# Twenty-six weight units of a dense expert layer: five closing additions and splits issued between second-layer tiles, with pinned queue order

## The chip, the cores and the metric

The kernel runs on one core of a Trainium2 chip. The metric is the device time of one execution in microseconds. The core has a TensorE (PE; its weight loads are shown apart as PEld), a VectorE (DVE), a ScalarE (ACT), a GpSimd (POOL) and a SyncE (SP), which here issues the loads from DRAM. Each engine works through a queue of its own in order.

## What is computed

The reference, cut to what matters:

```python
x = attention(q, k, v)                  # block-causal, 4 x 8 heads, 576 x 64 -> x: 2304 x 512
P = sinkhorn(exp(x @ w_gate))           # 2304 x 8, eight rounds of normalising
out = 0
for e in range(8):
    h = np.maximum(x @ w1[e], 0.0)      # 2304 x 512 @ 512 x 1024
    out += P[:, e:e + 1] * (h @ w2[e])  # 2304 x 1024 @ 1024 x 512
return soft_moe(out, phi, w1_2, w2_2)   # second expert layer, 32 slots
```

All is float32. The kernel reaches this accuracy with three matmuls for each product: every operand is split into a high part, rounded to the matmul's own type, and the rest, the low part (high x high, high x low, low x high).

## The kernel before, in words

The attention takes the first sixth of the time, the second expert layer the last 5%. Between them lies the dense expert layer, in 32 **units**: 8 experts, each with 4 quarters of 256 hidden columns. A unit loads a piece of `w1` (512 x 256) and of `w2` (256 x 512). The 2304 tokens stand in chunks 0 to 3 of 512 and chunk 4 of 256.

**Products.** From unit 5 on, layer one of chunks 0 to 3 is not done by 32 block products but by 26 products of fixed linear combinations (a fast matrix scheme). `ws` holds the 26 combinations of the tokens, made once: the lambdas of `rec` (line 795) and `lin` (798) issue 16 + 32 additions, through `tt` (790), alternately on DVE and POOL. For each unit 26 combinations of the weights, the **weight forms**, are made (`make`, 881): 8 are plain blocks of the raw weights, 18 are sums listed in `AT`. A plain form is an ACT copy (899), which rounds to the high part, and a POOL subtraction (900), which gives the low part. A form of `AT` has a POOL addition (898) ahead of these two. 16 places hold forms; a place comes free when the last product that uses it is issued.

`L1S` (928) is a generator that walks the list `IR`: `mm` is a product (three matmuls of 128 x 512, line 955) into one of the PSUM banks n0 to n5; `copy` an ACT copy (958); `add` and `addb` an addition (962), on DVE if an operand is in PSUM, else on POOL; `fin` splits a finished block of hidden values through the ReLU (`hsplit`, 918): ACT writes the high part (919), DVE the low part (920). The list ends with five outputs: (2,1), (2,0), (3,0), (3,1) and what they need. In the name (t, f), t is the chunk and f the half of the hidden columns.

**Order of a unit in the loop (1057 to 1075), u = 5 to 30.** First layer one of chunk 4 (`L1P`, 969: 24 matmuls of 256 columns), mixed with layer two of the previous unit's chunk 2. Then `stage_s` (1050): the 26 products mixed with layer two of chunk 4 and of the previous unit's chunk 3. Then layer two of chunks 0 and 1: eight **tiles** of six matmuls (`L2`, 184; matmul 203), each ended by a DVE accumulation into the output (213). During `stage_s` a tile's PSUM bank is m0 or m1 (`pair_`); after it the tiles turn through all eight banks, in the order of `bank` (65), so that a tile can draw one that a `fin` has yet to read.

**Loads.** One raw buffer, `r`, holds first the next unit's `w2` and then its `w1`. `raw_w2` (833) issues the load of `w2` after product 17; four pieces of `split_w2` (841, with `split_piece`, 114: an ACT copy and a DVE subtraction, line 121, both pinned) read it after products 22 to 25; `dma_w1` (850) then issues the load of `w1` on SP and puts 26 forms into the list of those to be made. Eight calls of `make` follow after the tiles, and one after each step of the next unit.

**What sets the order.** The instructions are traced in the program's order, but the framework's scheduler may put them into the queues in another one. `keep` (787) ties an instruction behind the one traced before it on its engine; it is an order only, without a wait. Pinned are the matmuls, the accumulations of 213, the splits of `w2`; not pinned before are the three instructions of a weight form, the copies, additions and splits of `L1S`.

**The last unit** (u = 31, lines 1077 to 1087) has the 26 products with the previous chunk 3; its eight plain forms are made anew after them, and its `L1P` stands later, after the loads of the last stage are issued (1221 to 1224).

Of the kernel before, what the change touches and what calls it, by code (L numbers as in the profile page):

```python
# [29 lines left out]
def f32(ap):  # L30
    return ap.bitcast(F32)
# [3 lines left out]
def attn_moe_softmoe_kernel(ctx: ExitStack, tc: tile.TileContext, qk1, q, k, v, wg, w1, w2, phi, m2w1, m2w2, cst, out):  # L35
    nc = tc.nc
# [622 lines left out]
    for t in (12, 14, 16):  # L659
# [110 lines left out]
    ]  # L770

# [18 lines left out]
    def tt(pool, **kw):  # L790
        r = (nc.gpsimd if pool else nc.vector).tensor_tensor(**kw)
        if not pool:
            keep(r)

    def rec(c, kt):
        return lambda: tt(kt % 2, out=ws[4 * kt + c], in0=f32(xs(xh, c, kt)), in1=f32(xs(xl, c, kt)), op=ALU.add)

    def lin(k):
        d, a, b, o = FT[k]
        return lambda: tt(k % 2, out=ws[d], in0=ws[a], in1=ws[b], op=ALU.add if o == "+" else ALU.subtract)  # L800

    tfree, gone = [], {}

# [67 lines left out]
    def unit(u, k):  # L871
        return rw[u][:, k % 4, 128 * (k // 4):128 * (k // 4) + 128]

    def forms_of(u, plain, last):
        for k in range(26):
            n = PA.count(k) * (not plain) + (k < 8) * (5 if plain else 0 if last else 1)
            if n:
                eu[u, k] = n
                aq.append((u, k))

    def make():
        if not aq or not efree:
            return
        u, k = aq.pop(0)
        q = efree.pop(0)
        h, lo = entry(q)
        ew[u, k] = (h, lo, q)
        if k < 8:
            src = unit(u, k)
        else:  # L890
            if not tmpw:
                tmpw.extend([const.tile([128, 512], F32, tag="wgx", name="st"), const.tile([128, 128], F32, name="st2")])
            d, ka, a, kb, b, o = AT[k - 8]

            def tv(j):
                return tmpw[j // 4][:, 128 * (j % 4):128 * (j % 4) + 128]
            src = tv(d)
            nc.gpsimd.tensor_tensor(out=src, in0=unit(u, a) if ka == "u" else tv(a), in1=unit(u, b) if kb == "u" else tv(b), op=ALU.add if o == "+" else ALU.subtract)  # L898
        nc.scalar.activation(out=h, in_=src, func=AF.Copy)  # L899
        nc.gpsimd.tensor_tensor(out=lo, in0=src, in1=f32(h), op=ALU.subtract)  # L900

    def make_all(u):
        while aq and aq[0][0] == u:
            assert efree
            make()
# [9 lines left out]
        if eu[u, k] == 0:  # L915
            efree.append(ew[u, k][2])

    def hsplit(h, lo, src):
        nc.scalar.activation(out=h, in_=src, func=AF.Relu)  # L919
        nc.vector.scalar_tensor_tensor(out=lo, in0=src, scalar=0.0, in1=f32(h), op0=ALU.max, op1=ALU.subtract)  # L920

    HT = [[(ua, "hh"), (ua, "hl")], [(pb, "hB0"), (pb, "hB1")], [(pb, "hD0"), (pb, "hD1")], [(pb, "hC0"), (pb, "hC1")]]
    w4 = const.tile([128, H_], F32, name="w4")
# [4 lines left out]
    def L1S(u, hb):  # L928
        bk, wk = {}, {}

        def v(q):
            if q[0] == "b":
                return bk[q[1]]
            _, t, f, k = q
            if t == 4:
                return w4
            if (t, k) not in wk:
                p, g = HT[t][k == "l"]
                wk[t, k] = p.tile([128, 2, H_], F32, tag=g, name="wk")
            return wk[t, k][:, f]  # L940
        r = []
        for o in IR + [("mm",)]:
            if o[0] == "mm":
                if r:
                    yield
                if len(o) == 1:
                    break
                r.append(o)
                _, n, b, st = o
                if st:  # L950
                    bk[b] = pm2.tile([128, 512], F32, tag=f"n{b}", name="s")
                wh, wl = wt_of(u, PA[n])
                xhv, xlv = XF[n]
                for m, (a, x) in enumerate(((wh, xhv), (wh, xlv), (wl, xhv))):
                    nc.tensor.matmul(bk[b], a, x, start=(st and m == 0), stop=(m == 2), skip_group_check=not st)  # L955
                used(u, PA[n])
            elif o[0] == "copy":
                nc.scalar.activation(out=v(("s",) + o[1]), in_=v(o[2]), func=AF.Copy, scale=float(o[3]))  # L958
            elif o[0] in ("add", "addb"):
                out_ = v(("s",) + o[1]) if o[0] == "add" else bk[o[1]]  # L960
                ps_ = o[2][0] == "b" or o[3][0] == "b"
                (nc.vector if ps_ else nc.gpsimd).tensor_tensor(out=out_, in0=v(o[2]), in1=v(o[3]), op=ALU.add if o[4] == "+" else ALU.subtract)  # L962
            else:
                t, f = o[1]
                if t not in hb:
                    hb[t] = h_new(t, F32R, "hf")
                hsplit(hb[t][0][:, f], hb[t][1][:, f], v(o[2]))

    def L1P(c, u, hs):
        hh, hl = hs  # L970
        n = CH[c]
        for f in range(2):
            o = bank("l1")
            for kt in range(KD):
                wh, wl = wt_of(u, 4 * f + kt)
                xhv, xlv = xs(xh, c, kt), xs(xl, c, kt)
                nc.tensor.matmul(o[:, 0:n], wh, xhv, start=(kt == 0), stop=False)
                nc.tensor.matmul(o[:, 0:n], wh, xlv, start=False, stop=False)  # L978
                nc.tensor.matmul(o[:, 0:n], wl, xhv, start=False, stop=(kt == KD - 1))  # L979
                used(u, 4 * f + kt)  # L980
                if kt == KD - 1:
                    hsplit(hh[:, f, 0:n], hl[:, f, 0:n], o[:, 0:n])
                yield

    def inter(g1, pend, pat, at=None):
        g2 = (y for x in pend for y in L2(*x))
        n = 0
# [12 lines left out]

# [46 lines left out]
    pair_ = [(pm, "m0"), (pm, "m1")]  # L1047
    all_ = list(banks)

    def stage_s(u, pend, pat, at):  # L1050
        hb = {}
        banks[:] = pair_
        inter(L1S(u, hb), pend, pat, at)
        banks[:] = all_
        return hb

    for u in range(5, NU - 1):
        i = ND + u - 4
        h4 = h_new(0, F32R, "h4")
        if u > 5:  # L1060
            inter(L1P(4, u, h4), [(i - 1, "2", hb[2])], PP[8])
            late_ = [(i - 1, "3", hb[3])]
        else:
            inter(L1P(4, u, h4), pend, "ll" + PP[4].replace("l", "", 2))
            late_ = []
        sw_ = split_w2(u + 1)
        at = {17: [lambda: make_all(u)] + raw_w2(u + 1), 22: sw_[0:1], 23: sw_[1:2], 24: sw_[2:3], 25: sw_[3:4], 26: dma_w1(u + 1)}
        hb = stage_s(u, [(i, "4", h4)] + late_, "lplplplp" + ("plppl" * 3 + "plplp" + "p" * 10 if late_ else "p" * 22), at)
        for c in range(2):
            for _ in L2(i, str(c), hb[c]):  # L1070
                pass
        for c in range(8):
# [148 lines left out]
    h4 = pb.tile([128, 2, 2, 256], F32R, tag="T12", name="h4")
    hl_all[4] = h4[:, 0], h4[:, 1]
    for _ in L1P(4, u, hl_all[4]):
        pass
# [273 lines left out]
```

## Time and profile before

| | us |
|---|---|
| median of 3 runs | 2080.23 (2078.78 to 2081.42) |
| the profiled execution | 2079.27 |
| its span in the profile | 2077.5 |
| PE busy | 1839.1 (89% of the span) |
| DVE busy | 1246.9 (60%) |
| POOL busy | 995.4 (48%) |
| ACT busy | 782.2 (38%) |

Busy times are times in which an engine executed something. PE's matmuls overlap in their pipeline, so a busy PE is not PE at its peak; its granted clock is shown apart, as a share of full speed. A row of a timeline gives start, length, engine, line, operation, output and inputs, and in brackets the idle time ahead of it on its engine with what ended it.

### The profile page before, as it was taken

To read this page: it belongs to the slowest core of one execution; us is meant where nothing else is said; L and a number is where in the kernel's file an instruction comes from. 1 tells how busy PE (TensorE), PEld (TensorE's weight loads), DVE (VectorE), ACT (ScalarE), POOL (GpSimd) and SP (SyncE) were. 2 spreads that over 40 slices of the span, in tenths; PEclk is the share of its full clock that TensorE was granted. 3 is DMA by queue.
4 is the path that set the end of the run, shared out by engine and by line. 5 is a ranking of instruction groups with operands and counts; after the bars stand their busy time and mean duration, and the time that the engine had idled before them with its cause. 6 is when DMAs were issued, how large, how long until landed. Compare 5 with 4: busy or idle time off the path is not lost.

```text
span 2077.5 us, 27268 instructions
## 1 busy us (share of the span) xinstructions
PE 1839.1 (89%) x9138; PEld 1411.9 (68%) x9138; DVE 1246.9 (60%) x2310; ACT 782.2 (38%) x2202; POOL 995.4 (48%) x1688
## 2 busy tenths in 40 slices
PE   9999999898889888888888889888888888889898
PEld 5666667786667767666666667766666666667664
DVE  6565555875655655566666656655565666666642
ACT  6666553263332323333333333333332333332332
POOL 4332224426554555555555555455555555554501
PEclk9999999999999999999999999999999999999999
DMA  6332210100000000000000000000000000000587
GB/s 199 102 102 94 66 53 30 42 11 21 21 21 21 21 20 11 21 21 11 21 21 21 21 21 21 21 21 11 21 21 11 21 21 21 21 21 21 192 294 257
DMA packets 79068, 103.14 MB, mean 50 GB/s; under 512 B 4689, under 2 KB 55633, under 8 KB 78929
## 3 DMA queue, kind: packets, MB, share of 16 engines
q1 hardware_dynamic: 78928, 101.42, 14.7%
q8 instruction: 72, 1.18, 0.2%
q14 instruction: 68, 0.55, 0.1%
HBM read 96.68 MB, written 4.72 MB: 49 GB/s over the span
## 4 chain that ended last, share of the span: by engine, by line
PE 58%; POOL 16%; DVE 12%; issue 4%; ACT 3%; DMA 3%; DVEq 0%; ACTq 0%; POOLq 0%; SPq 0%
PE l L203 30%; PE s L955 11%; POOL wk L962 7%; POOL es L900 6%; DVE wk L962 4%; POOL st L898 4%; DMA r<-in_moe_w_dram 3%; DVE w2l L121 2%; PE pvp L531 2%; PE tp L499 2%; DVE hf L920 2%; PE s L417 2%; ACT es L899 2%; PE l L978 2%; PE l L979 2%
## 5 line engine op out<-in xcount | busy, mean ns | idle before, releaser
L203 PE MATMUL l<-w2h,hf 128*128 128x512 f32 x1728 | 640.4, 418 | 181.5 <-DVE hf L920 180.2
L203 PEld LDWEIGHTS l<-w2h,hf 128*128 128x128 f32 x1728 | 350.8, 203 | 270.9 <-DVE hf L920 194.1
L213 DVE SCALAR_TENSOR_TENSOR acc<-l,P,acc 128x512 f32<-128x512 f32 x504 | 372.0, 748 | 231.1 <-PE l L203 229.9
L900 POOL TENSOR_TENSOR es<-st,es 128x128 fp32r<-128x128 f32 x486 | 218.1, 461 | 428.6 <-PE l L979 237.8
L203 PE MATMUL l<-w2l,hf 128*128 128x512 f32 x864 | 359.9, 417 | 0.0
L955 PE MATMUL s<-xh,es 128*128 128x512 f32 x864 | 327.1, 400 | 25.0 <-DVE hf L920 23.3
L899 ACT ACTIVATE es<-st 128x128 fp32r<-128x128 f32 x486 | 137.8, 306 | 466.0 <-PE l L978 317.4
L962 POOL TENSOR_TENSOR wk<-wk 128x512 f32<-128x512 f32 x189 | 244.1, 1310 | 133.2 <-DVE wk L962 133.0
L955 PE MATMUL s<-T,es 128*128 128x512 f32 x810 | 216.9, 393 | 5.9 <-DVE wk L962 3.1
L955 PEld LDWEIGHTS s<-xh,es 128*128 128x128 f32 x864 | 162.1, 188 | 86.5 <-DVE hf L920 45.9
L962 DVE TENSOR_TENSOR wk<-s,wk 128x512 f32<-128x512 f32 x216 | 148.6, 689 | 99.9 <-POOL wk L962 37.9
L203 PEld LDWEIGHTS l<-w2l,hf 128*128 128x128 f32 x864 | 177.6, 206 | 33.4 <-issue 0.2
L955 PEld LDWEIGHTS s<-T,es 128*128 128x128 f32 x810 | 150.0, 188 | 47.2 <-DVE wk L962 17.3
L962 DVE TENSOR_TENSOR s<-s,wk 128x512 f32<-128x512 f32 x162 | 110.9, 688 | 116.5 <-POOL wk L962 116.5
L955 PE MATMUL s<-xl,es 128*128 128x512 f32 x432 | 168.6, 390 | 0.0
L919 ACT ACTIVATE hf<-s 128x512 fp32r<-128x512 f32 x189 | 106.5, 594 | 157.8 <-DVE s L962 150.2
L920 DVE SCALAR_TENSOR_TENSOR hf<-s,hf 128x512 fp32r<-128x512 f32 x189 | 126.1, 680 | 45.4 <-ACT hf L919 45.4
L898 POOL TENSOR_TENSOR st<-r 128x128 f32<-128x128 f32 x162 | 72.6, 461 | 136.0 <-DMA r<-in_moe_w_dram 133.9
L475 POOL TENSOR_SCALAR pe<-pe,sm 128x384 f32<-128x384 f32 (+2 forms) x80 | 54.1, 680 | 143.2 <-DVE sm L462 65.0
L958 ACT ACTIVATE wk<-s 128x512 f32<-128x512 f32 x189 | 103.4, 593 | 17.5 <-PE s L955 16.8
L120 ACT ACTIVATE w2h<-r 128x256 fp32r<-128x256 f32 x160 | 54.1, 407 | 127.3 <-PE l L203 116.0
L900 POOL TENSOR_TENSOR es<-r,es 128x128 fp32r<-128x128 f32 x230 | 99.2, 470 | 4.4 <-ACT es L899 3.4
(252 smaller groups left out, 3108.2 us busy)
## 6 DMA issues: line engine op xcount, KB each, us to landing
r<-in_moe_w_dram SPq DMA_DIRECT2D x80, 512.0 KB, 3.4
mw<-in_moe_w_dram SPq DMA_DIRECT2D x64, 512.0 KB, 6.6
kraw<-in_k_dram SPq DMA_DIRECT2D x16, 576.0 KB, 3.9
qraw<-in_q_dram SPq DMA_DIRECT2D x16, 320.0 KB, 4.6
v<-in_v_dram SPq DMA_DIRECT2D x16, 256.0 KB, 3.0
out_dram<-ob SPq DMA_DIRECT2D x6, 512.0 KB, 3.5
out_dram<-ob SPq DMA_DIRECT2D x6, 256.0 KB, 2.3
qk<-in_qk_dram SPq DMA_DIRECT2D x4, 256.0 KB, 4.5
```

Source lines behind the costliest of these rows:

```text
L120: p = [nc.scalar.activation(out=h, in_=r[:, a:a + 256], func=AF.Copy)]
L203: nc.tensor.matmul(o, lh, w[:, kf, :], start=(m == 0), stop=(m == 5))
L213: nc.vector.scalar_tensor_tensor(out=av, in0=o, scalar=P[:, tt, e:e + 1], in1=av, op0=ALU.mult, op1=ALU.add)
L475: nc.gpsimd.tensor_scalar(out=p_[:, 0:n_], in0=p_[:, 0:n_], scalar1=sm[:, i:i + 1], scalar2=1.0, op0=ALU.mult, op1=ALU.mult)
L898: nc.gpsimd.tensor_tensor(out=src, in0=unit(u, a) if ka == "u" else tv(a), in1=unit(u, b) if kb == "u" else tv(b), op=ALU.add if o == "+" ...
L899: nc.scalar.activation(out=h, in_=src, func=AF.Copy)
L900: nc.gpsimd.tensor_tensor(out=lo, in0=src, in1=f32(h), op=ALU.subtract)
L919: nc.scalar.activation(out=h, in_=src, func=AF.Relu)
L920: nc.vector.scalar_tensor_tensor(out=lo, in0=src, scalar=0.0, in1=f32(h), op0=ALU.max, op1=ALU.subtract)
L955: nc.tensor.matmul(bk[b], a, x, start=(st and m == 0), stop=(m == 2), skip_group_check=not st)
L958: nc.scalar.activation(out=v(("s",) + o[1]), in_=v(o[2]), func=AF.Copy, scale=float(o[3]))
L962: (nc.vector if ps_ else nc.gpsimd).tensor_tensor(out=out_, in0=v(o[2]), in1=v(o[3]), op=ALU.add if o[4] == "+" else ALU.subtract)
```

## The change

The list `IR` gets a mark `("y",)`, at which `L1S` hands control back. The last product and the addition to bank n1 move ahead of the addition to bank n2, and a mark stands before each of the four last groups. `stage_s` takes the eight tiles of chunks 0 and 1 as a second generator and issues it by a pattern: "l" is half a tile, "y" one group of the list. While it does, the tiles turn through the banks m0, m1, n3, n4, n5 only. The four splits of `w2` move from products 22 to 25 to behind the second "l" (one tile); the load of `w1` and eight `make` calls stand at the pattern's end. All additions, copies and splits of `L1S` and all three instructions of `make` are pinned. The 48 additions of `rec` and `lin` all go to POOL, and are not pinned there. The mix of the unit's first stage has a new pattern. In the last unit `L1P` of chunk 4 takes the place of the tiles between the groups, and its plain forms are kept rather than made anew.

```diff
         ("add", (2, 1, "l"), ("s", 3, 1, "l"), ("s", 2, 1, "h"), "+"),
         ("add", (3, 0, "h"), ("s", 2, 0, "h"), ("s", 2, 1, "h"), "+"),
+        ("mm", 25, 1, True),
+        ("addb", 1, ("b", 1), ("s", 4, 0, "h"), "+"),
+        ("y",),
         ("addb", 2, ("b", 2), ("s", 2, 1, "l"), "+"),
         ("fin", (2, 1), ("b", 2)),
+        ("y",),
         ("fin", (2, 0), ("s", 3, 0, "h")),
-        ("mm", 25, 1, True),
-        ("addb", 1, ("b", 1), ("s", 4, 0, "h"), "+"),
+        ("y",),
         ("fin", (3, 0), ("b", 0)),
+        ("y",),
         ("fin", (3, 1), ("b", 1)),
...
-        return lambda: tt(k % 2, out=ws[d], in0=ws[a], in1=ws[b], op=ALU.add if o == "+" else ALU.subtract)
+        return lambda: tt(1, out=ws[d], in0=ws[a], in1=ws[b], op=ALU.add if o == "+" else ALU.subtract)
...
-            n = PA.count(k) * (not plain) + (k < 8) * (5 if plain else 0 if last else 1)
+            n = PA.count(k) * (not plain) + (k < 8) * (5 if plain else 1)
...
-        nc.scalar.activation(out=h, in_=src, func=AF.Copy)
-        nc.gpsimd.tensor_tensor(out=lo, in0=src, in1=f32(h), op=ALU.subtract)
+        keep(nc.scalar.activation(out=h, in_=src, func=AF.Copy))
+        keep(nc.gpsimd.tensor_tensor(out=lo, in0=src, in1=f32(h), op=ALU.subtract))
...
-    def stage_s(u, pend, pat, at):
+    def stage_s(u, pend, pat, at, fill_, fpat, hooks):
         hb = {}
+        g = L1S(u, hb)
         banks[:] = pair_
-        inter(L1S(u, hb), pend, pat, at)
+        inter(g, pend, pat, at, True)
+        banks[:] = [b for b in all_ if b[1] not in ("n0", "n1", "n2")]
+        f = fill_(hb)
+        n = 0
+        for ch in fpat:
+            next(g if ch == "y" else f, None)
+            n += 1
+            for x in hooks.get(n, ()):
+                x()
+        for x in (g, f):
+            for _ in x:
+                pass
         banks[:] = all_
...
-            inter(L1P(4, u, h4), [(i - 1, "2", hb[2])], PP[8])
+            inter(L1P(4, u, h4), [(i - 1, "2", hb[2])], "llll" + "p" * 8 + "llll")
...
-        sw_ = split_w2(u + 1)
-        at = {17: [lambda: make_all(u)] + raw_w2(u + 1), 22: sw_[0:1], 23: sw_[1:2], 24: sw_[2:3], 25: sw_[3:4], 26: dma_w1(u + 1)}
...
+        at = {17: [lambda: make_all(u)] + raw_w2(u + 1)}
+        after = dma_w1(u + 1)[0]
...
+            l2s, "llllyllyllyllyl", {2: split_w2(u + 1), 15: [after] + [make] * 8},
...
+    hb = stage_s(u, [(last_i - 1, "3", hb[3])], "plppl" * 4 + "p" * 14, {}, last_p, "ppppypypypypp", {})
     assert not aq and not aux
-    for k in range(8):
-        ew.pop((u, k), None)
-        eu[u, k] = 1
-        aq.append((u, k))
-    for k in range(8):
-        make()
```

## Rows read from the trace of the kernel before

**Rows 1.** The page: span and busy time of each engine

```profile
span 2077.5 us, 27268 instructions
PE 1839.1 (89%) x9138; PEld 1411.9 (68%) x9138; DVE 1246.9 (60%) x2310; ACT 782.2 (38%) x2202; POOL 995.4 (48%) x1688
```

**Rows 2.** PE's timeline: the first tile's start, and waits in units 6, 15, 30

```profile
566.22 0.79 PE L203 MATMUL l<-w2h,hf 128*128 128x512 f32 x1 [6.92 <-DVE hf L920]
...
1062.85 0.40 PE L203 MATMUL l<-w2h,hf 128*128 128x512 f32 x1
...
1076.40 0.80 PE L203 MATMUL l<-w2h,hf 128*128 128x512 f32 x1 [7.04 <-DVE hf L920]
...
1925.32 0.80 PE L203 MATMUL l<-w2h,hf 128*128 128x512 f32 x1 [6.18 <-DVE hf L920]
```

**Rows 3.** Waits of PE: idle us, count, longest

```profile
PE l L203 <- DVE hf L920: 180.2, 27, 7.2
```

**Rows 4.** Stretches: length, busy PE, PEld, DVE, ACT, POOL, granted clock, DMA share, GB/s

```profile
566.22:1925.32 1359.10, 1167.13 (x5040) 934.20 (x5040) 822.45 (x1225) 441.65 (x1198) 738.38 (x1271) 0.93 0.06 19
1019.37:1076.40 57.03, 48.97 (x210) 39.20 (x210) 34.31 (x52) 18.43 (x51) 30.80 (x54) 0.92 0.06 19
1076.40:1079.50 3.10, 3.10 (x8) 2.50 (x9) 1.93 (x4) 0.20 (x1) 1.29 (x4) 0.54 0.02 5
1079.50:1083.00 3.50, 3.50 (x19) 2.93 (x18) 2.89 (x5) 0.00 (x0) 0.00 (x0) 1.00 0.00 0
```

**Rows 5.** POOL's timeline ahead of the wait that ends at 1076.40

```profile
1063.10 0.89 POOL L898 TENSOR_TENSOR st<-r 128x128 f32<-128x128 f32 x2 [5.05 <-DMA r<-in_moe_w_dram]
...
1065.20 3.40 POOL L900 TENSOR_TENSOR es<-r,es 128x128 fp32r<-128x128 f32 x8
...
1069.40 2.48 POOL L962 TENSOR_TENSOR wk<-wk 128x512 f32<-128x512 f32 x2
```

**Rows 6.** The chain that ended last, around the products: start, length, what

```profile
1035.83 0.69 PE s L955 x3
```

**Rows 7.** DVE's timeline, and ACT's, at the end of a unit's products

```profile
1058.25 0.69 DVE L962 TENSOR_TENSOR s<-s,wk 128x512 f32<-128x512 f32 x1
...
1060.12 0.68 DVE L920 SCALAR_TENSOR_TENSOR hf<-s,hf 128x512 fp32r<-128x512 f32 x1
...
1065.50 0.74 DVE L213 SCALAR_TENSOR_TENSOR acc<-l,P,acc 128x512 f32<-128x512 f32 x1
...
1060.24 0.60 ACT L919 ACTIVATE hf<-s 128x512 fp32r<-128x512 f32 x1 [0.59 <-DVE s L962]
```

**Rows 8.** DVE's timeline: the splits of `w2`, two and two

```profile
1056.34 1.99 DVE L121 TENSOR_TENSOR w2l<-r,w2h 128x256 fp32r<-128x256 f32 x2
...
1058.85 0.74 DVE L121 TENSOR_TENSOR w2l<-r,w2h 128x256 fp32r<-128x256 f32 x2
```

**Rows 9.** SP's timeline: the load of `w1`

```profile
1059.62 0.37 SPq L854 DMA_DIRECT2D r<-in_moe_w_dram  x1
```

**Rows 10.** Timelines: forms of `AT`, at 1093 on POOL, at 1151 on all engines

```profile
1093.12 0.46 POOL L898 TENSOR_TENSOR st<-st,r 128x128 f32<-128x128 f32 x1
...
1094.42 0.46 POOL L898 TENSOR_TENSOR st<-r 128x128 f32<-128x128 f32 x1
...
1151.36 0.46 POOL L898 TENSOR_TENSOR st<-r 128x128 f32<-128x128 f32 x1
...
1152.79 0.46 POOL L898 TENSOR_TENSOR st<-st 128x128 f32<-128x128 f32 x1
```

**Rows 11.** Additions of `rec` and `lin`: ns min/median/max, first and last start

```profile
L791 POOL TENSOR_TENSOR wT<-wT,wT x12: 1262/1292/2034, 343.1 to 417.2; 128x512 f32<-128x512 f32 x12
L791 DVE TENSOR_TENSOR wT<-wT,wT x9: 676/683/1153, 367.8 to 416.5; 128x512 f32<-128x512 f32 x9
```

**Rows 12.** The last unit: PE's timeline, and the stretch behind its wait, columns as in group 4

```profile
1969.83 0.38 PE L977 MATMUL l<-xh,es 128*128 128x256 f32 x1 [2.37 <-DVE hf L920]
...
1969.80:1973.00 3.20, 3.17 (x14) 3.08 (x15) 2.19 (x5) 0.87 (x2) 0.00 (x0) 0.55 1.01 340
```

More of the change, by code (lines that the diff above doesn't have):

```diff
@@ L795, in rec @@
     def rec(c, kt):
-        return lambda: tt(kt % 2, out=ws[4 * kt + c], in0=f32(xs(xh, c, kt)), in1=f32(xs(xl, c, kt)), op=ALU.add)
+        return lambda: tt(1, out=ws[4 * kt + c], in0=f32(xs(xh, c, kt)), in1=f32(xs(xl, c, kt)), op=ALU.add)
     def lin(k):
         d, a, b, o = FT[k]
-        return lambda: tt(k % 2, out=ws[d], in0=ws[a], in1=ws[b], op=ALU.add if o == "+" else ALU.subtract)
+        return lambda: tt(1, out=ws[d], in0=ws[a], in1=ws[b], op=ALU.add if o == "+" else ALU.subtract)
     tfree, gone = [], {}
@@ L897, in make @@
             src = tv(d)
-            nc.gpsimd.tensor_tensor(out=src, in0=unit(u, a) if ka == "u" else tv(a), in1=unit(u, b) if kb == "u" else tv(b), op=ALU.add if o == "+" else ALU.subtract)
-        nc.scalar.activation(out=h, in_=src, func=AF.Copy)
-        nc.gpsimd.tensor_tensor(out=lo, in0=src, in1=f32(h), op=ALU.subtract)
+            keep(nc.gpsimd.tensor_tensor(out=src, in0=unit(u, a) if ka == "u" else tv(a), in1=unit(u, b) if kb == "u" else tv(b), op=ALU.add if o == "+" else ALU.subtract))
+        keep(nc.scalar.activation(out=h, in_=src, func=AF.Copy))
+        keep(nc.gpsimd.tensor_tensor(out=lo, in0=src, in1=f32(h), op=ALU.subtract))
     def make_all(u):
@@ L916, in used, with hsplit @@
             efree.append(ew[u, k][2])
-    def hsplit(h, lo, src):
-        nc.scalar.activation(out=h, in_=src, func=AF.Relu)
-        nc.vector.scalar_tensor_tensor(out=lo, in0=src, scalar=0.0, in1=f32(h), op0=ALU.max, op1=ALU.subtract)
+    def hsplit(h, lo, src, pin=False):
+        p = [nc.scalar.activation(out=h, in_=src, func=AF.Relu)]
+        p.append(nc.vector.scalar_tensor_tensor(out=lo, in0=src, scalar=0.0, in1=f32(h), op0=ALU.max, op1=ALU.subtract))
+        for x in p if pin else ():
+            keep(x)
     HT = [[(ua, "hh"), (ua, "hl")], [(pb, "hB0"), (pb, "hB1")], [(pb, "hD0"), (pb, "hD1")], [(pb, "hC0"), (pb, "hC1")]]
@@ L942, in L1S @@
         for o in IR + [("mm",)]:
-            if o[0] == "mm":
+            if o[0] == "y":
+                yield
+            elif o[0] == "mm":
                 if r:
@@ L957, in L1S @@
             elif o[0] == "copy":
-                nc.scalar.activation(out=v(("s",) + o[1]), in_=v(o[2]), func=AF.Copy, scale=float(o[3]))
+                keep(nc.scalar.activation(out=v(("s",) + o[1]), in_=v(o[2]), func=AF.Copy, scale=float(o[3])))
             elif o[0] in ("add", "addb"):
@@ L961, in L1S @@
                 ps_ = o[2][0] == "b" or o[3][0] == "b"
-                (nc.vector if ps_ else nc.gpsimd).tensor_tensor(out=out_, in0=v(o[2]), in1=v(o[3]), op=ALU.add if o[4] == "+" else ALU.subtract)
+                keep((nc.vector if ps_ else nc.gpsimd).tensor_tensor(out=out_, in0=v(o[2]), in1=v(o[3]), op=ALU.add if o[4] == "+" else ALU.subtract))
             else:
@@ L966, in L1S @@
                     hb[t] = h_new(t, F32R, "hf")
-                hsplit(hb[t][0][:, f], hb[t][1][:, f], v(o[2]))
+                hsplit(hb[t][0][:, f], hb[t][1][:, f], v(o[2]), True)
     def L1P(c, u, hs):
@@ L983, in L1P, with inter @@
                 yield
-    def inter(g1, pend, pat, at=None):
+    def inter(g1, pend, pat, at=None, part=False):
         g2 = (y for x in pend for y in L2(*x))
@@ L996, in inter @@
                     f()
-        for g in (g2, g1):
+        for g in (g2,) if part else (g2, g1):
             for _ in g:
@@ L1065, in attn_moe_softmoe_kernel, with l2s @@
             late_ = []
-        sw_ = split_w2(u + 1)
-        at = {17: [lambda: make_all(u)] + raw_w2(u + 1), 22: sw_[0:1], 23: sw_[1:2], 24: sw_[2:3], 25: sw_[3:4], 26: dma_w1(u + 1)}
[L1068 to L1072, printed above, removed]
-            make()
+        at = {17: [lambda: make_all(u)] + raw_w2(u + 1)}
+        after = dma_w1(u + 1)[0]
+        def l2s(hb):
+            for c in range(2):
+                yield from L2(i, str(c), hb[c])
+        hb = stage_s(
+            u, [(i, "4", h4)] + late_, "lplplplp" + ("plppl" * 3 + "plplp" + "p" * 10 if late_ else "p" * 22), at,
+            l2s, "llllyllyllyllyl", {2: split_w2(u + 1), 15: [after] + [make] * 8},
+        )
     u = NU - 1
@@ L1079, in attn_moe_softmoe_kernel, with last_p @@
         pass
-    hb = stage_s(u, [(last_i - 1, "3", hb[3])], "plppl" * 4 + "p" * 14, {})
-    assert not aq and not aux
-    for k in range(8):
-        ew.pop((u, k), None)
-        eu[u, k] = 1
-        aq.append((u, k))
-    for k in range(8):
-        make()
+    h4 = []
+    def last_p(hb):
+        t = pb.tile([128, 2, 2, 256], F32R, tag="T12", name="h4")
+        h4.extend([t[:, 0], t[:, 1]])
+        return L1P(4, u, h4)
+    hb = stage_s(u, [(last_i - 1, "3", hb[3])], "plppl" * 4 + "p" * 14, {}, last_p, "ppppypypypypp", {})
+    assert not aq and not aux
     A = const.tile([128, DM], F32, tag="wgx", name="A")
@@ L1220, in attn_moe_softmoe_kernel @@
     load_w([(xp, f"{a}{c}{k}") for c in (0, 1, 3) for a in ("xh", "xl") for k in range(2)] + [(xp, "xh21"), (xp, "xl21")] + [(pb, t) for t in ("T00", "T01", "T02", "T20", "T21", "T30", "T31")] + [(wp, f"w2h{1 - lp}")])
[L1221 to L1224, printed above, removed]
+    hl_all[4] = h4
     load_w([(xp, "xh40"), (xp, "xl40"), (wp, "r")] + [(wp, t) for t in ETAG])
```

## The prediction, made blind

> **What bounds the kernel now.** I start with the page: PE is busy for 89% of the span, POOL for 48% [rows 1]. The reader is to see that no engine is full, so that the order of waits decides. Next comes PE's timeline: once a unit, at the tiles of chunk 0, it shows PE idle for 6 to 7 us until a DVE split of hidden values is done, 25 times from 566.22 to 1925.32 [rows 2]. PE's waits add these up: 27 of that kind cost 180.2 us [rows 3]. The 24 periods between these take 1359.10 us, 56.63 each, and PE is not the limit in them: in the one from 1019.37 it is busy for 48.97 us, POOL for 30.80 [rows 4].
>
> What makes PE wait is in POOL's queue [rows 5]. The outputs (2,1) and (3,0) need two POOL additions; these start at 1069.40 and take 2.48 us, and PE runs on at 1076.40. Ahead of them POOL had waited 5.05 us for the load of `w1`, then made weight forms from 1063.10 on, which the products of the next unit need only later. The tiles of chunk 0 draw, after five tiles, a PSUM bank that a late split has yet to read, and PE stands for 7.04 us. Behind that it runs at a granted clock of 0.54 for 3.10 us, thus near 1.2 GHz, before the next stretch shows 1.00 [rows 4]: about 1.4 us more. One unit's wait costs 8.4 us.
>
> **What the change does, part by part**, for one unit of the loop. T0 is the end of the last product's issue (1062.85 before [rows 2]).
>
> *Taken away:* pinned additions come before the next unit's forms, so POOL can't put forms ahead of them, and the 8.4 us go. If nothing were late next, a unit would be PE's own work: 186 matmuls of 512 columns at 0.227 us (three in 0.68 to 0.69 [rows 6]) and 24 of 256 at 0.12, 45.0 us.
>
> *What is late next: the first tile.* 444 PSUM tiles are drawn before the first unit's tiles, and the count modulo five is the same in every unit: tile 0 draws n5 of the five-bank list. n5 is freed by the DVE subtraction (2,1,h) of product 24, and in the pinned queue this stands behind four groups of addition, ReLU on ACT, low part on DVE, which no longer overlap: 0.69 + 0.11 + 0.60 + 0.11 + 0.60 = 2.1 us each, from the DVE and ACT rows (issue spacing 0.60; 0.11 for a hand-over is my estimate from them) [rows 7]. Four take 8.4 from the end of product 17; the next addition and the subtraction end at 9.7; products 18 to 25 take 8 x 0.68 = 5.4 of that [rows 6]. So tile 0 starts at T0 + 4.3. Before, it started at once.
>
> *The load of `w1`.* The splits of `w2`, which free the raw buffer, are now pinned behind tile 0's accumulation: T0 + 4.3 + 1.4 (six matmuls) + 0.75 for the accumulation and 0.75 of its wait [rows 7] + 1.5 for four splits (two in 0.74 [rows 8]) = T0 + 8.7. The ACT halves overlap. The load itself takes 3.48, from issue at 1059.62 [rows 9] to POOL's start at 1063.10 [rows 5]. Forms start at L = T0 + 12.2; before, at T0 + 0.25. SP carries only the two loads of a unit here, so nothing is behind them on its queue. The load of `w2` keeps its place and is covered by eight products.
>
> *The forms, now in strict order.* First the eight plain ones: 3.40 for eight subtractions [rows 5] + 0.4 for the first copy, 3.8. Each form of `AT` is a round trip: POOL adds, ACT copies, POOL subtracts, and pinned, the next addition can't slip in between. A trip is 1.30 to 1.43 in the rows [rows 10]; I take 1.36, the middle. Product 10 needs an ACT copy of an earlier product and is issued behind the last forms, so 17 trips are in its way, 23.1 us; the 18th gives 0.9 more; two POOL additions of `IR` lie between, 2.6 (1.29 each in the POOL row of the same shape [rows 11]). L + 30.4. Then the chain from product 10's copy: ACT 0.7, DVE 0.8, two POOL additions 2.6 (2.48 and a hand-over [rows 5]), DVE 0.8, together 4.9, after which products 15 to 25 take 11 x 0.68 = 7.5 [rows 6]. The next T0 is at L + 42.8.
>
> Sum: 12.2 + 42.8 = 55.0. I add 1.0 for PE's clock behind the new gap of 4.3 us and for splits of `w2` that meet a POOL addition. Its bounds: 0, and 1.4 (the slow stretch of [rows 4]) + 1.25 (1.99 against 0.74 for two splits [rows 8]) = 2.65. So **56.0 us a unit against 56.63**, over 25 units 16 us.
>
> At the splits a rule speaks against the change. Two of them took 1.99 us while POOL worked and 0.74 when POOL was idle [rows 5, 8]. The Trainium skill, page "SBUF — State Buffer", section "Who interferes with whom", says that a DVE instruction with two SBUF inputs contends with a GpSimd instruction that reads SBUF. The rows agree with it. By the rule the splits, moved next to the two pinned POOL additions, would lengthen each time they meet, and the sum would be 57.25 where it is now 56.0.
>
> *The small parts.* The 48 additions of `rec` and `lin` on POOL: 48 x 1.29 = 62 us, against 74 us from the first to the last of those that POOL does now [rows 11], so the units of plain products that run there hide them, and DVE is relieved of 24 x 0.68. If that cover fails, POOL's other work there (splits of weights) waits: 0 +- 3 us. The new mix of chunk 4 with chunk 2 only reorders work that PE does anyway: between -0.5 and +0.5 a unit, taken as 0, since forms are the limit then. In the last unit `L1P` fills the gap of 2.37 us and 1.5 us of slow clock behind it (3.20 us at 0.55) go [rows 12]: -4.
>
> **Sum.** the profiled execution, 2079.27 (a span of 2077.5 and 1.8 around it), gives 2079.27 - 16 - 4 = 2059; it lies 1 us below the median of 2080.23, so I forecast 2060.
>
> **Rivals.**
> - *Round trips at the dear end* (slower). At 1.43 instead of 1.36 the 17 trips take 1.2 us more, 57.2 a unit: +14 - 4, 2090; with split collisions of 1 us a unit on top, 2115. The turning point is at a trip of 1.40 us: beyond it the strict order of the forms costs more than the wait of PE that is removed. For it: 1.43 in the quiet stretch at 1151 [rows 10], and ACT also has copies of products pinned between. Against it: 1.30 at 1093.
> - *Tile 0 doesn't wait for n5, or the `w1` load goes 2.5 us earlier* (DVE's groups overlap better than I count, or the scheduler places splits ahead of the accumulation): 53.5 a unit, -78 - 4, 2000. For it: DVE's rows at the end show the groups interleaved before, 0.6 us apart [rows 7]. Against it: the pins write the order out.
> - *Forms are no limit at all* (places are free early, forms run far ahead of their products): PE's 45.0 + 1.5, 46.5 a unit, 1823. Against it: a form needs the load, which comes 12 us later than before.
> - *Nothing changes:* another late operation keeps PE waiting as long (the accumulation, or bank n4 in place of n2), 56.6 a unit: 2080 within 4 us.
>
> **How the numbers follow.** My sum: 0.42, with its own range of 2035 to 2075. Dear trips: 0.27. Earlier load: 0.13. PE as the limit: 0.06. No change: 0.12. The range leaves out 1823 and the outer ends: 1998 to 2112. It is wide because a unit's 0.1 us is 2.5 us of the whole, and the trip's bounds of 1.30 and 1.43 alone span 55 us. Within 0.2%, 4 us, a measurement of this kernel can't tell a difference from none. Faster 0.42 + 0.13 + 0.06 = 0.61, the same 0.12, slower 0.27.
>
> **What the profile of the changed kernel would show.** If right: two POOL additions directly behind the subtraction of product 24 and no form ahead of them; a PE wait of about 4 us at tile 0, released by DVE line 962's subtraction; `w1` issued some 9 us behind the last product; POOL's forms one by one at 1.36 us; then PE waits of several us in the products 10 to 15, released by POOL or ACT. Wrong: PE waits stay behind tile 4 (no change), trips at 1.43 or longer (slower rival), the `w1` load within 6 us of the last product (faster rival), PE busy above 95% of a unit (forms no limit).

## The result and the profile after

The changed kernel takes 2046.04 us (median; 2042.42 to 2047.44) against 2079.93 for the kernel before on the same chip: a ratio of 0.9834, 95% interval 0.9817 to 0.9851. The forecast was 2060 in a range of 1998 to 2112. Direction and range held. The working did not: the 34 us are what is left of a gain of 83 us in the loop, which the forecast had put at 16, after losses of some 50 us, of which it had none.

The page of the changed kernel, its head:

```profile
span 2045.7 us, 27013 instructions
...
PE 1835.8 (90%) x9138; PEld 1368.5 (67%) x9138; DVE 1229.0 (60%) x2286; ACT 787.6 (39%) x2196; POOL 1016.5 (50%) x1706
```

PE has the same work as before [rows 1] in a shorter span. Its waits, the view of [rows 3]:

```profile
PE s L963 <- DVE wk L970: 61.5, 50, 1.7
PE gm L307 <- DVE mbg L303: 38.3, 1, 38.3
PE s L963 <- DVE hf L924: 28.1, 47, 1.0
...
PE l L203 <- DVE hf L924: 1.4, 2, 1.1
```

The wait that the change was about, 180.2 us in 27 pieces, is 1.4 us. What is new is one wait of 38.3 us, ahead of the loop, on line 303, which the diff doesn't touch. Two stretches show both sides (columns as in [rows 4]): 24 periods of the loop, from the end of unit 6's products to that of unit 30's, and the new wait:

```profile
599.35:1876.52 1277.17, 1150.99 (x5041) 889.25 (x5040) 788.77 (x1224) 448.62 (x1201) 738.34 (x1272) 1.00 0.06 20
...
350.50:388.50 38.00, 0.29 (x2) 0.00 (x0) 38.00 (x1) 0.60 (x1) 38.00 (x32) 0.54 0.00 0
```

A unit takes 1277.17 / 24 = **53.22 us** in place of 56.63, at a granted clock of 1.00 in place of 0.93. Where the time went is read by setting the last product of each unit beside the same matmul of the kernel before. At unit 5 the changed kernel is 46.8 us late (34 at its first product, 13 more in its products). From there to unit 30 it gains 82.8 us, 3.31 a unit. In the last unit it loses 3.1 us and behind it another 1.1, and ends 31.8 us ahead in span.

**The wait of 38.3 us.** DVE's timeline of the changed kernel:

```profile
349.47 0.30 DVE L301 TENSOR_REDUCE m<-P 128x1 f32<-128x144 f32 x1
349.69 0.42 DVE L179 SCALAR_TENSOR_TENSOR hl<-l,hh 128x256 fp32r<-128x256 f32 x1
350.02 38.92 DVE L303 COPY mbg<-m 128x128 f32<-128x128 f32 x1
```

A copy that takes 0.22 us in the kernel before is shown as running for 38.92. It copies the gate's maximum, from SBUF to SBUF; PE transposes the result, so PE stands too. Beside it, POOL:

```profile
386.38 1.26 POOL L795 TENSOR_TENSOR whD<-wT,whD 128x512 f32<-128x512 f32 x1
387.60 1.26 POOL L795 TENSOR_TENSOR whC<-wT,whC 128x512 f32<-128x512 f32 x1
388.93 2.62 POOL L795 TENSOR_TENSOR wT<-wT,wT 128x512 f32<-128x512 f32 x2
```

These are the 48 additions of `rec` and `lin`. From 351.04 on, each starts 1.22 us after the one before and overlaps its end by 0.04; at 388.93 the spacing is 1.33 for the first time, and there the copy ends (388.94). Whether this gap let the copy in or came from it isn't shown.

**The unit.** The end of the products, on PE (the view of [rows 2]):

```profile
1078.09 0.39 PE L963 MATMUL s<-xh,es 128*128 128x512 f32 x1
1078.32 0.39 PE L203 MATMUL l<-w2h,hf 128*128 128x512 f32 x1
```

The tiles start at once, at T0 = 1078.32, where a gap of 4.3 us was forecast. The subtraction that frees n5, the bank of tile 0, ends when the forecast has it, at T0 + 4.3 (1082.64):

```profile
1081.96 0.68 DVE L970 TENSOR_TENSOR wk<-s,wk 128x512 f32<-128x512 f32 x1
```

DVE at the splits of `w2` (the view of [rows 8]) and SP at the load of `w1` [rows 9]:

```profile
1071.57 1.89 DVE L121 TENSOR_TENSOR w2l<-r,w2h 128x256 fp32r<-128x256 f32 x2
...
1073.98 0.74 DVE L121 TENSOR_TENSOR w2l<-r,w2h 128x256 fp32r<-128x256 f32 x2
```

```profile
1074.75 0.37 SPq L858 DMA_DIRECT2D r<-in_moe_w_dram  x1
```

The splits run before the tiles, and the load is issued 3.6 us ahead of T0, not 8.7 behind it. What the forms then wait for shows on ACT and POOL, one unit earlier (T0 = 1025.12):

```profile
1034.15 1.09 ACT L923 ACTIVATE hf<-s 128x512 fp32r<-128x512 f32 x2 [0.87 <-DVE hf L924]
1035.12 1.70 ACT L903 ACTIVATE es<-r 128x128 fp32r<-128x128 f32 x8
```

```profile
1029.60 2.54 POOL L970 TENSOR_TENSOR wk<-wk 128x512 f32<-128x512 f32 x2 [9.61 <-DVE wk L970]
1035.51 3.40 POOL L904 TENSOR_TENSOR es<-r,es 128x128 fp32r<-128x128 f32 x8 [3.37 <-ACT es L903]
1038.87 0.46 POOL L902 TENSOR_TENSOR st<-r 128x128 f32<-128x128 f32 x1
1039.75 0.47 POOL L904 TENSOR_TENSOR es<-st,es 128x128 fp32r<-128x128 f32 x1 [0.42 <-ACT es L903]
1040.17 0.47 POOL L902 TENSOR_TENSOR st<-r,st 128x128 f32<-128x128 f32 x1
...
1064.32 0.46 POOL L904 TENSOR_TENSOR es<-st,es 128x128 fp32r<-128x128 f32 x1 [0.42 <-ACT es L903]
```

The two additions now come before any form, where [rows 5] had them behind. The pinned ACT copies of the forms stand behind the last two ReLUs: ACT begins them at T0 + 10.0, and POOL waits for ACT, not for a DMA. A round trip, addition to addition, is 1040.17 - 1038.87 = 1.30 us. The last form ends at 1064.78, 29.7 us behind the first ACT copy, and the next T0 comes 13.5 us later.

### The profile page after: what moved, and what is told of

Read it like the earlier page. It is cut to its first block, busy times and chain, and to the rows that moved or that the text cites. A ratio compares the mean times of both kernels' runs of the same rounds, so it can differ in the third digit from the quotient of the medians.

```text
span 2045.7 us, 27013 instructions
## 1 busy us (share of the span) xinstructions
PE 1835.8 (90%) x9138; PEld 1368.5 (67%) x9138; DVE 1229.0 (60%) x2286; ACT 787.6 (39%) x2196; POOL 1016.5 (50%) x1706
## 4 chain that ended last, share of the span: by engine, by line
PE 32%; POOL 28%; DVE 21%; issue 10%; ACT 7%; POOLq 0%; DMA 0%; ACTq 0%; DVEq 0%
PE l L203 13%; POOL es L904 11%; POOL st L902 8%; POOL wk L970 5%; DVE s L970 5%; DVE wk L970 4%; DVE acc L213 4%; POOL w L970 3%; DVE hf L924 3%; ACT hf L923 3%; DVE w2l L121 2%; PE pvp L531 2%; DVE mbg L303 2%; PE tp L499 2%; PE s L417 2%
## 5 line engine op out<-in xcount | busy, mean ns | idle before, releaser
L203 PE MATMUL l<-w2h,hf 128*128 128x512 f32 x1728 | 588.6, 395 | 9.3 <-DVE acc L213 7.5
L963 PE MATMUL s<-xh,es 128*128 128x512 f32 x864 | 340.9, 416 | 63.5 <-DVE hf L924 28.1
L203 PEld LDWEIGHTS l<-w2h,hf 128*128 128x128 f32 x1728 | 324.9, 188 | 95.6 <-DVE acc L213 18.5
L203 PE MATMUL l<-w2l,hf 128*128 128x512 f32 x864 | 338.0, 391 | 0.0
L903 ACT ACTIVATE es<-st 128x128 fp32r<-128x128 f32 x486 | 150.9, 311 | 456.8 <-POOL st L902 454.9
L963 PE MATMUL s<-T,es 128*128 128x512 f32 x810 | 229.0, 408 | 48.6 <-DVE wk L970 41.7
L203 PEld LDWEIGHTS l<-w2l,hf 128*128 128x128 f32 x864 | 162.6, 188 | 30.8
L970 DVE TENSOR_TENSOR wk<-wk,s 128x512 f32<-128x512 f32 x81 | 55.7, 688 | 126.1 <-POOL w L970 90.4
L203 PE MATMUL l<-w2h,h 128*128 128x512 f32 x216 | 87.4, 406 | 30.4 <-ACT h L923 16.3
L924 DVE SCALAR_TENSOR_TENSOR h<-l,h 128x256 fp32r<-128x256 f32 x54 | 22.9, 424 | 149.1 <-ACT h L923 149.1
```

Of the source, the lines that this page charges most:

```text
L203: nc.tensor.matmul(o, lh, w[:, kf, :], start=(m == 0), stop=(m == 5))
L903: keep(nc.scalar.activation(out=h, in_=src, func=AF.Copy))
L924: p.append(nc.vector.scalar_tensor_tensor(out=lo, in0=src, scalar=0.0, in1=f32(h), op0=ALU.max, op1=ALU.subtract))
L970: keep((nc.vector if ps_ else nc.gpsimd).tensor_tensor(out=out_, in0=v(o[2]), in1=v(o[3]), op=ALU.add if o[4] == "+" else ALU.subtract))
```

## The experiments

All runs keep the reference's whole computation. A unit's time is the stretch of 24 periods, taken as above. The times of e1, e2 and e12 are medians of four runs, those of the others single runs; seven runs of the kernel before, beside e1, lie between 2075.05 and 2082.45 us.

### The additions on POOL

**e1**, the changed kernel with the additions alternating again:

```diff
-        return lambda: tt(1, out=ws[d], in0=ws[a], ...
+        return lambda: tt(k % 2, out=ws[d], in0=ws[a], ...
```

(and the same in `rec`).

> The changed kernel with one part undone: the 48 additions of rec and lin alternate again between DVE and POOL. Theory A (these additions, back to back on POOL, hold up the one DVE copy of the gate's maximum for 38.92 us, and PE behind it): the copy takes 0.2 us again, PE's wait of 38.3 us goes, and with it some 3 us of slow clock; 2046 - 41 = 2005, between 1998 and 2012. Theory B (the copy was late for another reason, such as the order in which the attention ends): the wait stays, 2046 within 5. In both the unit of the loop stays at 53.2 us.

2016.02 us (ratio to before 0.9692, 0.9675 to 0.971). The copy on DVE:

```profile
350.80 0.22 DVE L303 COPY mbg<-m 128x128 f32<-128x128 f32 x1
```

Theory A holds; its size doesn't: 30 us came back, not 41, and 2016 lies above its range. Part of the rest is known: the kernel with shared additions has waits of its own at that place (3.22 and 1.03 us of PE on the normalising's sums at 389.71 and 409.54), which the run on POOL is rid of. The unit stays at 53.29.

**e3**, the kernel before with all additions on POOL and nothing else:

> The kernel before with one part of the change alone: the 48 additions of rec and lin all on POOL. Theory A: the DVE copy takes some 38 us there too, the time is 2080 + 41 = 2121, between 2112 and 2128, and the units' period stays 56.6. Theory B (it takes the other parts to bring the stall about): 2080 within 5.

2108.28 us beside 2078.21 for the kernel before: 30 us again, under the forecast of 34 to 50. The line's own view, and the loop:

```profile
L303 DVE COPY mbg<-m x1: 38975/38975/38975, 349.9 to 349.9; 128x128 f32<-128x128 f32 x1
```

```profile
585.10:1942.08 1356.98, 1164.77 (x5041) 932.58 (x5040) 822.44 (x1225) 442.41 (x1201) 739.98 (x1272) 0.93 0.06 19
```

So this part alone brings the stall about, and it leaves the unit where it was (56.54). From two sides it costs 30 us.

**e2**, all additions on POOL, the copy on ACT:

```diff
-        nc.vector.tensor_copy(out=mbt[0], in_=m1.to_broadcast([128, 128]))
+        nc.scalar.activation(out=mbt[0], in_=m1.to_broadcast([128, 128]), func=AF.Copy)
```

> The changed kernel with all additions on POOL as they are, but the copy of the gate's maximum made by ACT in place of DVE. Theory A1 (what is held up is this DVE copy itself, by a conflict with POOL): the copy takes under 0.5 us, PE's wait of 38 us goes, 2005, between 1998 and 2015; DVE's instructions with two SBUF inputs may run longer beside POOL, for a few us. Theory A2 (POOL's run of additions holds up any instruction that follows there, by their order or a semaphore): ACT's copy or the one behind it waits as long, 2046 within 6.

2046.99 us: nothing won. That is A2's figure, but not its account: ACT's copy took 0.31 us, and the next DVE instructions ran as usual, up to line 314:

```profile
352.44 0.30 DVE L313 TENSOR_REDUCE rs<-P 128x18 f32<-128x144 f32 x1 [0.53 <-ACT P L309]
352.78 36.91 DVE L314 TENSOR_SCALAR rs<-rs 128x18 f32<-128x18 f32 x1
```

An instruction on 18 columns took 36.91 us. Both theories as written fall. What remained was that some forms of DVE instructions get no turn beside POOL's run. **e12** tested which:

```diff
-        nc.vector.tensor_scalar(out=rs, in0=rs, scalar1=1e-9, scalar2=None, op0=ALU.add)
+        nc.vector.scalar_tensor_tensor(out=rs, in0=rs, scalar=1e-9, in1=rs, op0=ALU.add, op1=ALU.max)
```

(the same in line 325, and the copy on ACT as in e2).

> The changed kernel with all 48 additions on POOL as they are; the copy of the gate's maximum on ACT, and in the normalising the two DVE instructions of the form TENSOR_SCALAR that read SBUF (lines 314 and 325) written as SCALAR_TENSOR_TENSOR with the same values. Theory C (a copy or TENSOR_SCALAR of DVE from SBUF gets no turn while POOL's additions follow on one another; forms like TENSOR_REDUCE and SCALAR_TENSOR_TENSOR do): no DVE instruction of the normalising runs over 3 us, PE's wait of 37 to 38 us is gone, 2046 - 33 = 2013, between 2003 and 2022. Theory D (after the copy some instruction of DVE always waits for the end of POOL's run, whatever its form): the long one is RECIPROCAL or the new form, 2047 within 4.

2045.05 us (0.9845, 0.9828 to 0.9861).

```profile
352.37 0.30 DVE L313 TENSOR_REDUCE rs<-P 128x18 f32<-128x144 f32 x1 [0.53 <-ACT P L309]
352.71 36.88 DVE L314 SCALAR_TENSOR_TENSOR rs<-rs 128x18 f32<-128x18 f32 x1
```

Theory C falls in its list of forms: this SCALAR_TENSOR_TENSOR waits as long. It reads both inputs from SBUF; those of line 179, which ran in 0.42 us in the same stretch, read one from PSUM. So a copy from SBUF, a TENSOR_SCALAR from SBUF and an instruction with two inputs from SBUF have been seen to wait out POOL's run, and reductions, and instructions with an input from PSUM, not to. Theory D's figure came, with the new form as the long one; its "whatever its form" goes too far, since a reduction passed just ahead (352.37). RECIPROCAL was never the first in line beside POOL's run, so D isn't excluded for it; later in e2 one took 0.20 us (from 392.49) inside a POOL instruction (392.29 to 393.02). No run took all the waiting forms off DVE, so it isn't shown that PE's wait would then go. The Trainium skill, page "SBUF — State Buffer", section "Who interferes with whom", tells of a port pair that DVE and GpSimd share as an exclusive lock and counts copies, TENSOR_SCALAR and instructions with two SBUF inputs among those that can contend. The rows agree, though no run here tests the port itself. The page speaks of blocking for one instruction; here it lasted for thirty.

### What sets the unit

These kernels start from e1, apart from e5. The kernel before took 2084.45 us beside e5 to e8.

**e4** pins the splits of `w2` where the prediction had taken them to be pinned, behind tile 0's accumulation:

```diff
-        if (pc >= 4 or i < 2) and i < len(inst) and inst[i][1] is not None:
+        if (pc >= 4 and i >= ND_ + 2) or ((pc >= 4 or i < 2) and i < len(inst) and inst[i][1] is not None):
```

> As the first kernel of this call, and the four splits of w2 of each unit pinned behind tile 0's accumulation, as the prediction took them to be. Theory A (the prediction's walk was right but for this order): the w1 load is issued about 9 us behind the last product in place of 3.5 us ahead of it, forms start at T0 + 12.5 in place of T0 + 10.0, the unit takes 55.7 in place of 53.2 us and the whole about 2005 + 62 = 2067, between 2045 and 2075. Theory B (the load isn't what the forms wait for, ACT's order behind the last ReLUs is, and there is room in it): 2005 within 8.

2084.6 us. From T0 = 1019.84 on: the load on SP, the first ACT copies of forms, POOL's last form, the next T0; and the loop:

```profile
1029.01 0.37 SPq L858 DMA_DIRECT2D r<-in_moe_w_dram  x1
```

```profile
1032.20 1.71 ACT L903 ACTIVATE es<-r 128x128 fp32r<-128x128 f32 x8 [0.91 <-DMA r<-in_moe_w_dram]
```

```profile
1062.80 0.46 POOL L904 TENSOR_TENSOR es<-st,es 128x128 fp32r<-128x128 f32 x1 [0.42 <-ACT es L903]
```

```profile
1075.68 0.39 PE L203 MATMUL l<-w2h,hf 128*128 128x512 f32 x1
```

```profile
570.37:1913.60 1343.23, 1190.21 (x5041) 919.82 (x5040) 764.83 (x1224) 450.99 (x1201) 735.46 (x1272) 0.96 0.06 19
```

The load goes out at T0 + 9.2, the unit takes 55.97. Theory A holds: 69 us over e1, forecast 62. The whole lies outside its range of 2045 to 2075, which started from 2005 instead of e1's 2016. Forms now wait for the load and start at T0 + 12.4; the last one ends 31.1 us later (1063.26), and the next T0 comes 12.4 us behind that, where the changed kernel takes 13.5.

**e5** is the kernel before with the pins alone (the `keep` lines of the diff), **e6** is e1 without them.

> The kernel before with the pins alone: additions, copies and splits of L1S and the forms pinned in issue order; the five outputs, the tiles, the load of w1 and rec and lin where they were. Theory A (the pins remove the wait, since they put the two POOL additions ahead of the forms; moving the outputs between tiles is worth little): PE's wait of 7 us falls under 2.5 us, the unit takes 53 to 54.5 us, the whole 2010 to 2035 with some 12 us lost in the first unit as in the changed kernel. Theory B (the pins serialise the ends without the tiles between them, so the wait stays): 56 to 58 a unit, 2070 to 2120.

> The kernel of e1 without the pins: outputs issued between the tiles, five banks for the tiles, rec and lin shared by DVE and POOL, but the forms, additions, copies and splits not pinned. Theory A (the forms go ahead of the additions again, yet no tile draws the banks that wait, so PE has cover, and the forms start at T0 instead of T0 + 10): 47 to 52 us a unit, 1880 to 1985. Theory B (late outputs then keep PE waiting elsewhere, in the next unit's chunk 2 or at the end of the tiles): 55 to 58 a unit, 2060 to 2130.

e5: 1990.51 us. e6: 1970.73. Their loops, e5 and e6:

```profile
564.82:1813.99 1249.17, 1150.31 (x5041) 893.21 (x5040) 797.46 (x1225) 449.55 (x1201) 741.43 (x1272) 1.00 0.07 21
```

```profile
551.58:1810.59 1259.01, 1151.42 (x5041) 917.15 (x5040) 795.50 (x1225) 443.42 (x1201) 743.92 (x1272) 0.97 0.07 21
```

52.05 and 52.46 us a unit: **either part alone does more than both together** (53.29 in e1). e5 came out better than its theory A; e6 lies just above its theory A in the unit and within it in the whole. With the pins alone, the last ReLUs come earlier in ACT's queue, and the forms with them (T0 = 1033.79):

```profile
1040.59 1.09 ACT L919 ACTIVATE hf<-s 128x512 fp32r<-128x512 f32 x2 [0.84 <-DVE hf L920]
1041.56 1.70 ACT L899 ACTIVATE es<-r 128x128 fp32r<-128x128 f32 x8
```

That is T0 + 7.8 against T0 + 10.0. In e6 the forms again stand ahead of the additions, as theory A says:

```profile
1029.29 2.49 POOL L968 TENSOR_TENSOR wk<-wk 128x512 f32<-128x512 f32 x2
```

That is T0 + 6.5, as late as before [rows 5]; but the tiles no longer draw the banks that wait for them, and PE's wait there is 2.2 us, on an accumulation. Over the run:

```profile
PE l L203 <- DVE acc L213: 80.9, 38, 2.4
```

In e6 PE is idle for 4.5 us a unit (1259.01 - 1151.42, over 24), and these waits, over the 26 units of the loop, make some 3.1 of them: forms are not what PE waits for there. Unit 5's products took 26 us there and 38 with the pins: the loss of 13 us in the first unit is that of pinned forms.

**e7** issues the load of `w1` and the plain forms behind the splits (`{2: split_w2(u + 1) + [after] + [make] * 8}`), so that their ACT copies stand ahead of the last ReLUs:

> The kernel of e1 with the load of w1 and the eight plain forms issued behind the splits, after the second half tile, in place of the end of the tiles: their ACT copies come ahead of the last four ReLUs, their POOL subtractions right behind the two additions. Theory A (the forms' chain sets the unit, and it starts when ACT has done the last ReLU, 10 us behind the last product): it starts some 3.4 us earlier, 49.8 a unit, 2016 - 85 = 1931, between 1915 and 1955. Theory B (the chain isn't what the unit waits for): 2016 within 8.

1969.77 us; the loop, ACT and POOL (T0 = 1027.94):

```profile
563.37:1801.31 1237.94, 1145.38 (x5041) 891.20 (x5040) 799.15 (x1224) 449.32 (x1200) 749.70 (x1272) 1.00 0.07 21
```

```profile
1027.76 0.31 ACT L903 ACTIVATE es<-r 128x128 fp32r<-128x128 f32 x1 [1.40 <-DMA r<-in_moe_w_dram]
```

```profile
1035.08 3.84 POOL L904 TENSOR_TENSOR es<-r,es 128x128 fp32r<-128x128 f32 x8
...
1050.87 0.46 POOL L904 TENSOR_TENSOR es<-st,es 128x128 fp32r<-128x128 f32 x1 [1.13 <-PE s L963]
...
1053.07 1.29 POOL L970 TENSOR_TENSOR w<-w,wk 128x512 f32<-128x512 f32 x1 [0.44 <-DVE wk L970]
```

51.58 a unit, between the theories: POOL's forms begin 3.3 us earlier against T0 (at T0 + 7.1 in place of T0 + 10.4), and the unit is 1.7 shorter. POOL's rows show where the rest goes: the eight subtractions take 3.84 in place of 3.40, one subtraction waits for 1.13 in place of 0.42, and one addition waits for DVE for 0.44, together 1.6 lost.

**e8** issues the POOL subtraction of each form of `AT` behind the next form's addition:

```diff
-        keep(nc.gpsimd.tensor_tensor(out=lo, in0=src, in1=f32(h), op=ALU.subtract))
+        flush_lo()
+        lows.append(((u, k), lambda: keep(nc.gpsimd.tensor_tensor(out=lo, in0=src, in1=f32(h), op=ALU.subtract))))
+        if k < 8 or k == 25:
+            flush_lo()
...
```

(`flush_lo` issues what `lows` holds; a product that needs a form issues its subtraction first.)

> The kernel of e1 with each AT form's POOL subtraction issued behind the next form's POOL addition, so that POOL works while ACT copies. Theory A (the chain of 18 round trips of 1.30 us sets the unit): a trip takes about 0.9 us, forms end 7 us earlier, the unit falls to 46.5 to 48.5, where PE is the limit; 2016 - 25 x 5.7 = 1873, between 1845 and 1910. Theory B (POOL's trips are covered): 2016 within 8.

1902.68 us. POOL's timeline and the loop:

```profile
1011.91 0.48 POOL L908 TENSOR_TENSOR st<-r 128x128 f32<-128x128 f32 x1
1012.47 0.46 POOL L908 TENSOR_TENSOR st<-r,st 128x128 f32<-128x128 f32 x1
1012.89 0.46 POOL L911 TENSOR_TENSOR es<-st,es 128x128 fp32r<-128x128 f32 x1
1013.31 0.46 POOL L908 TENSOR_TENSOR st<-r,st 128x128 f32<-128x128 f32 x1
```

```profile
555.15:1736.27 1181.12, 1120.78 (x5041) 894.92 (x5040) 792.57 (x1224) 443.10 (x1201) 727.88 (x1272) 1.00 0.07 22
```

A form takes 0.84 us in place of 1.30, with no wait for ACT, and the unit 49.21. PE is busy for 95% of it. Theory A holds within its total; the unit stays 0.7 above its range.

### A version that beats both

**e9** joins e8 and e7 and leaves the forms of units 4 and 5 unpinned; **e10** puts e8's order and the unpinned forms on e5; **e11** is e9 with the last unit's forms unpinned too. Beside the edits shown, e9 has this one:

```diff
         u, k = aq.pop(0)
+        pin = (lambda x: x) if u <= 5 else keep
```

> A search for a version that beats both: the kernel of e8, with the load of w1 and the plain forms issued early as in e7, and the forms of units 4 and 5 not pinned. If forms still hold up the unit by the 1.5 to 2 us that e8 leaves above PE's 46.5, the unit falls from 49.2 to 47 to 48.5; unpinned forms in unit 5 give back the 8 us that the first unit lost. 1903 - 25 - 8 = 1870, between 1850 and 1895. If e8 is already at PE's limit: 1895 within 6.

> The other structure: the kernel of e5 (pins alone, the five outputs and the tiles where they were before) with the form order of e8 and the forms of units 4 and 5 not pinned. If the order of the forms is what counts and moving the outputs between tiles is worth nothing, 52.05 falls to 47.5 to 49 a unit, 1990 - 25 x 3.8 - 8 = 1887, between 1865 and 1910; if the outputs issued between the tiles cover something once forms are short, it stays above 50, over 1930.

> As e9, and the forms of the last unit not pinned either. The last unit's products took 34 us in e8 and 25 in e6, where forms were free: if its pinned forms are the cause, 7 to 9 us less than e9; if free forms go ahead of unit 30's two POOL additions and bring the wait of 7 us back once, within 3 us of e9.

e9: 1883.97 us, e10: 1895.2, e11: 1885.69, beside 2083.95 for the kernel before. The loops of e9 and e10:

```profile
547.02:1719.79 1172.77, 1121.15 (x5041) 894.27 (x5040) 801.50 (x1224) 441.09 (x1202) 738.44 (x1272) 1.00 0.07 22
```

```profile
544.59:1721.57 1176.98, 1122.21 (x5041) 897.03 (x5040) 799.77 (x1225) 438.05 (x1201) 727.93 (x1272) 1.00 0.07 22
```

48.87 and 49.04: with e8's order the two structures are 0.2 us a unit apart, and starting the forms early, e9 against e8, is worth 0.3. e9 is within its range and 14 above its figure: of the two terms the first unit gave its share back (unit 5 is 1.7 us behind the kernel before, in place of 9.2 in e8), the loop did not. Of e10's 11 us over e9, 9.3 are one PE wait on the last unit's ReLUs; e9, with `L1P` between them, has 3.2 there. e11 came out as its second case, with one wait of 6.9 us ahead of the last unit. e9 is 200 us faster than the kernel before and 162 faster than the changed one.

## Why the prediction came out as it did

**The bound.** That late additions made PE wait, and that the forms' queue made them late, held: pinned, they are in front, and the wait is gone, with the pins alone too (e5). That the chain of forms is what then sets the unit held too: e8 shortens nothing else and takes 4 us off a unit, and e4 starts the forms 2.4 us later and adds 2.7.

**Tile 0 waits for n5 (T0 + 4.3): failed.** The matmuls and the accumulations of line 213 are not pinned; the section on the kernel before says that they are, and the code doesn't. n5 came free at T0 + 4.3, as the walk has it; but in PE's queue, as the program is built, the scheduler put the three other tiles of chunk 0 and two matmuls of chunk 1 ahead of tile 0, 20 matmuls or some 4.5 us (20 x 0.227), and PE went on at once.

**The load of `w1` at T0 + 8.7: failed**, for the same kind of reason. The pin in `split_piece` hangs on `inst[i][1] is not None`, and the units of the loop stand in that list with None. The splits are free, ran before the tiles, and the load was issued at T0 - 3.6. e4 pins them: the load goes to T0 + 9.2 and the unit to 55.97, where the forecast had 8.7 and 56.0. Leg by leg (start of the forms, forms, from the last form to the next T0) e4 has 12.4, 31.1 and 12.4 us, the walk 12.2, 30.4 and 12.4 and 1.0 of allowance. Apart from tile 0, the walk was right for a kernel with that pin.

**The start of the forms.** L was T0 + 12.2 by the load; measured T0 + 10.0, by ACT's order behind the last ReLUs, which the walk had not looked at: 2.2 us less a unit. **The forms:** the plain ones took the 3.8 forecast (0.4 for the first copy, 3.40 for POOL). A trip was taken at 1.36, measured 1.30, the lower bound: 1.0 over 17 trips. All forms together took 29.7 in place of 30.4. **The last leg** took 13.5, where the sum has 12.4 and an allowance of 1.0 for slow clock and for splits of `w2` that meet a POOL addition. The clock had no part (the loop shows 1.00), the splits had: in every unit two take 1.9 us beside POOL's additions, as before the change [rows 8], in front of the additions and ReLUs on which PE then waits (28.1 us in 47 waits). In e4, whose splits come later, the leg is 12.4. So the two splits did lengthen, as the rule in the prediction has it, but within the allowance and not on top of the sum. In all 53.2 where 56.0 stood, the figure of the second rival (53.5), by both its causes: PE doesn't stand at tile 0, and the load goes early, with the sign that was set for it.

**The additions of `rec` and `lin`, 0 +- 3: failed**, the largest single miss. Their time was costed against a window, and the cover was said to be the units of plain products. They cost 30 us (e1, e3), and not by POOL's own lateness, but because a DVE instruction (the copy, or in e2 and e12 the one of line 314) had no turn beside them. The two bounds asked only what waits for POOL, not what works beside it. The row that could have warned was [rows 8]: 1.99 us for two splits beside POOL, against 0.74, which the prediction used for the splits alone.

**Left out:** the first unit. Its forms are pinned too: 13 us lost, most of which e9 gives back by leaving them unpinned. **The last unit, -4: failed**, +4 (3.1 in it, 1.1 behind it): PE waits there for forms, as at

```profile
1902.22 0.50 PE L963 MATMUL s<-xh,es 128*128 128x512 f32 x1 [1.95 <-ACT es L903]
```

since they too start behind unit 30's last ReLUs, with only chunk 2 to cover them. Unpinned (e11), they bring one wait of 6.9 us in their place. The new mix of chunk 4 with chunk 2, taken as 0, was not tested by itself.

So it is luck that 2060 lay near 2046: an underrated gain (83 for 16) met unseen losses (34 up to unit 5, of which the additions are 30, 13 in unit 5, 4 at the end).

## What to carry to other kernels

Before walking a queue by hand, read for each instruction in it whether the pin is executed there, not only whether it is written: one condition moved a load by 13 us (e4 against the changed kernel). When work is moved to another engine, ask what runs beside it, not only who waits for it: a run of additions without a gap held a tiny instruction of another engine for 37 to 39 us here. And a chain of round trips between two engines can be shortened by its issue order: one instruction moved behind the next form's addition was worth 4 us a unit, more than any other single edit to e1 here.

## What was not expected of the hardware

DVE instructions on 18 and 128 columns stood for 36.9 and 38.9 us beside some thirty POOL additions that followed on one another 1.22 us apart, and ended at the first longer spacing (1.33 in the changed kernel). Reductions, and instructions with an input from PSUM, passed in 0.2 to 0.7 us in the same run. The profile shows the wait as busy time: DVE reads 38.00 of 38.00 us in that stretch, and no row names POOL.
